# Where the gate's two halves lie in their slot, and the order of the products that read them

## The chip, the cores and the metric

The kernel runs on one core of a Trainium2 chip. Its metric is the device time of one execution in microseconds (us). Before the change three runs took 2553.76, 2554.19 and 2555.51 us; the median is 2554.19 us. The profile shown here is of a separate execution that took 2554.62 us.

## The reference

The program does two things one after the other, in float32. First a spectral layer on x of shape 8 x 3008 x 256: a Fourier transform along the 3008 positions, a complex 256 x 256 mix of the channels with a bias, a soft threshold, and the transform back. Then a feed-forward layer on the 24,064 resulting tokens:

```
h = x @ w_in                      # 256 -> 2048
relu6 = np.clip(h + 3.0, 0.0, 6.0)
g = h * relu6 / 6.0               # the gate
out = g @ w_out                   # 2048 -> 256
```

The change is in the last line of this layer, `g @ w_out`.

## The kernel before, in words

To keep float32 precision on TensorE the kernel splits both factors of most matrix products in two: a high part (the value rounded to the type `float32r`) and a low part (what is left). One product is then three matmuls that add into the same PSUM bank: weights low times data high, weights high times data high, weights high times data low. `product` (L133) writes these three in one of two orders. With `later=True` the matmul on the low part of the data comes last. Without it, it is the second of the three.

The tokens are cut into 47 chunks of T = 512 and the 2048 hidden features into 8 blocks of 256, which gives 376 units (a chunk and a block each). A unit goes through these steps, interleaved with those of its neighbours and with the spectral layer's work for later chunks (lists of slots written before the loop decide what is laid where, and `in_order` and `behind` hold some of it in that order; the rest is ordered by the framework's scheduler):

- the products with `w_in` on 256 columns of tokens (`block`, data in `yb`, weights in `w_in_hi` and `w_in_lo`, results in `pb` and `ps_a`). A Strassen-like scheme turns 8 of them into 7;
- the gate (`gate`, L1077 to L1106): ScalarE computes relu(h + 3) (L1099), VectorE min(.., 6) * h into `r` (L1101), ScalarE rounds `r` to the high part (L1104, two instructions of 512 columns), VectorE subtracts to get the low part (L1105, one instruction of 1024 columns);
- four groups of the products with `w_out` (`down`, L1108): for each of the two halves u of the block and the two halves dh of the 256 outputs one group of three matmuls on 512 columns, with the data in `gs` and the sums in `po`. All 8 blocks of a chunk add into the same two banks.

`gate_parts` (L1077) makes the slot of `gs`: 4T + 64 elements of 4 bytes in each partition, two such slots in turn. In it the high part starts at element 60 (byte 240) and the low part at element 2T + 60 (byte 4336). Both are 112 bytes past a multiple of 128.

In the program as built, the two slots of `gs` and all slots of `yb` start at multiples of 128 bytes; so do the moving operands of the products with `w_in`. The weights `w_in` and `w_out` start 64 bytes past such a multiple, and since a block of 128 weights has 512 bytes, so does each block. For two other groups of three matmuls on 512 columns: `z` (both parts) starts 64 bytes past, with the weights `g64` on a multiple; `xs` (both parts) starts on a multiple, with the weights `f47` 32 and 96 bytes past.

Of the kernel before, what the change touches and what calls it, by code (L numbers as in the profile page):

```python
# [32 lines left out]
T = 512  # L33
# [68 lines left out]
def spectral_ffn(ctx: ExitStack, tc: tile.TileContext, x, w_r, w_i, bias, w_in, w_out, f47, f64, g64, g64u, sgn, out):  # L102
# [11 lines left out]
    def space(shape, dt, name, tag=None):  # L114
        tag = tag or name
        return sb.tile(shape, dt, name=name, tag=tag, bufs=depth.get(tag, 1))
# [16 lines left out]
    def product(ps, terms, start=True, stop=True, more=False, later=False):  # L133

        todo = [p for (ah, al), (bh, bl) in terms for p in (((al, bh), (ah, bh), (ah, bl)) if later else ((al, bh), (ah, bl), (ah, bh)))]
        for n, (a, b) in enumerate(todo):
            nc.tensor.matmul(  # L137
                out=ps,
                lhsT=a,
                rhs=b,  # L140
                start=start and n == 0,
                stop=stop and n == len(todo) - 1,
                skip_group_check=more,
            )
# [590 lines left out]
    def part(pair, sl):  # L735
        return tuple(t[:, sl] for t in pair)
# [339 lines left out]

    def gate_parts(i):  # L1077

        starts = 60, 2 * T + 60
        t = space([P, 4 * T + 64], F32R, "gs")  # L1080
        return [t[:, at : at + 2 * T].rearrange("p (u c) -> p u c", u=2) for at in starts]

    def gate(i):

        h = hs.pop(i)
        if i == len(units) - 1:
            r = space([P, 2, T], F32, "r")
            t = gs[i] = gate_parts(i)
            for u in (1, 0):
                nc.scalar.activation(out=r[:, u], in_=h[:, u], func=AF.Relu, bias=three, scale=1.0)  # L1090
                nc.vector.scalar_tensor_tensor(
                    out=r[:, u], in0=r[:, u], scalar=6.0, in1=h[:, u], op0=ALU.min, op1=ALU.mult
                )
                split(t[0][:, u], t[1][:, u], r[:, u])
            yield
            return
        r = space([P, 2, T], F32, "r")
        for u in range(2):
            nc.scalar.activation(out=r[:, u], in_=h[:, u], func=AF.Relu, bias=three, scale=1.0)  # L1099
        yield  # L1100
        nc.vector.scalar_tensor_tensor(out=r, in0=r, scalar=6.0, in1=h, op0=ALU.min, op1=ALU.mult)  # L1101
        t = gs[i] = gate_parts(i)
        for u in range(2):
            nc.scalar.copy(out=t[0][:, u], in_=r[:, u])  # L1104
        nc.vector.tensor_tensor(out=t[1], in0=r, in1=t[0].bitcast(F32), op=ALU.subtract)  # L1105
        yield  # L1106

    def down(i, u, dh):  # L1108
        c, f = units[i]
        ft = 2 * f + u  # L1110
        ends = i == len(units) - 1
        first, last = f == 0 and u == 0, f == nf - 1 and u == (0 if ends else 1)
        if first:
            pos[dh] = ps_o.tile([P, 512], F32, name=f"po{dh}")
        g = gs[i]
        product(
            pos[dh],
            later=True,
            terms=[(part(wout_s, slice(ft * D + dh * P, ft * D + (dh + 1) * P)), (g[0][:, u], g[1][:, u]))],
            start=first,  # L1120
            stop=last,
        )
        if last:
            ot = space([P, T], F32, "ot")
            if ends and dh:
                for n, at in enumerate((slice(0, H), slice(H, T))):
                    if n:
                        nc.vector.tensor_scalar(
                            out=ot[:, at], in0=pos[dh][:, at], scalar1=1.0 / 6.0, scalar2=None, op0=ALU.mult
                        )  # L1130
                    else:
                        nc.scalar.mul(out=ot[:, at], in_=pos[dh][:, at], mul=1.0 / 6.0)
                    nc.sync.dma_start(
                        out=out[dh * P : (dh + 1) * P, c * T + n * H : c * T + (n + 1) * H], in_=ot[:, at]
                    )
                return
            if dh:
                nc.vector.tensor_scalar(out=ot, in0=pos[dh], scalar1=1.0 / 6.0, scalar2=None, op0=ALU.mult)
            else:
                nc.scalar.mul(out=ot, in_=pos[dh], mul=1.0 / 6.0)  # L1140
            nc.sync.dma_start(out=out[dh * P : (dh + 1) * P, c * T : (c + 1) * T], in_=ot)
# [134 lines left out]
    def group(i, at):  # L1276
        if 0 <= i < n:
            down(i, *order(i)[at])
# [71 lines left out]
```

## Time and profile before

| | |
|---|---|
| median of three runs | 2554.19 us |
| the profiled execution | 2554.62 us |
| its span, first to last instruction | 2552.8 us |
| PE (TensorE matmul) busy | 2532.1 us, 99% |
| DVE (VectorE) busy | 1958.1 us, 77% |
| ACT (ScalarE) busy | 1955.7 us, 77% |
| matmuls on `gs` (L137, into `po`) | 4512, 38% of the chain that ended last |

How to read it: a matmul's record begins when it starts and ends some time after the next one has begun, since matmuls are pipelined. The price of a matmul is therefore the distance from its start to the next start, not the length of its record. In a timeline, rows of the same kind are merged ("x2"), and the starts are given to 0.01 us; over a group of three or six matmuls that is fine enough.

### The profile page before, as it was taken

The numbers are of one execution on the slowest core, as the hardware profiler recorded it, in microseconds if no ns is written. First come the engines' busy times: TensorE is split into PE (matmuls) and PEld (weight loads), VectorE is DVE, ScalarE is ACT, GpSimd is POOL, SyncE is SP. The second block draws the span as 40 slices with busy tenths as digits, with TensorE's granted clock in tenths as the row PEclk, the third lists the DMA queues.
The fourth block names the chain that finished last, engine by engine and source line by source line (L and its number), as shares of the span: only waits on it lengthen the run. The fifth ranks groups of instructions, "written<-read, shape, count | busy, mean of one in ns | idle before, by whom it ended". The sixth has DMA issues, their size and how long they took to land.

```text
span 2552.8 us, 45563 instructions
## 1 busy us (share of the span) xinstructions
PE 2532.1 (99%) x16510; PEld 2260.0 (89%) x16510; DVE 1958.1 (77%) x3176; ACT 1955.7 (77%) x4329; POOL 738.3 (29%) x716
## 2 busy tenths in 40 slices
PE   9999999999999999999999999999999999999999
PEld 6788889899999889988899888998989999998988
DVE  6988877777777877777777777777777877777676
ACT  5777777777777777777777777777777777777877
POOL 2223423343133331433313432134311221121210
PEclk9999999999999999999999999999999999999999
DMA  8534422232122221232212322222311121110000
GB/s 277 174 101 134 132 74 72 82 95 75 56 83 80 89 81 52 81 84 80 82 55 77 92 88 67 65 78 82 91 60 60 56 70 54 37 32 25 20 17 17
DMA packets 147321, 199.75 MB, mean 78 GB/s; under 512 B 16319, under 2 KB 102039, under 8 KB 147095
## 3 DMA queue, kind: packets, MB, share of 16 engines
q1 hardware_dynamic: 147095, 196.83, 25.5%
q8 instruction: 130, 2.13, 0.3%
q14 instruction: 96, 0.79, 0.1%
HBM read 99.77 MB, written 74.97 MB: 68 GB/s over the span
## 4 chain that ended last, share of the span: by engine, by line
PE 89%; DVE 4%; ACT 3%; issue 2%; DMA 1%; POOL 0%; SPq 0%; DVEq 0%; ACTq 0%; POOLq 0%
PE po L137 38%; PE ps_a L137 24%; PE pb L137 19%; PE ps_a L871 3%; PE ps_a L757 2%; PE ps_a L472 1%; DVE gs L1105 1%; ACT gs L1104 1%; DVE r L1101 1%; DVE h L1014 1%; ACT r L1099 1%; DMA xin<-in_x 1%; PE ps_a L507 0%; PE pb L438 0%; DVE tc L796 0%
## 5 line engine op out<-in xcount | busy, mean ns | idle before, releaser
L137 PE MATMUL po<-gs,w_out_hi 128*128 128x512 f32 x3008 | 948.1, 395 | 1.1 <-DVE gs L1105 1.0
L1099 ACT ACTIVATE r<-h,three 128x512 f32<-128x512 f32 x750 | 541.7, 726 | 147.5 <-DVE h L1014 132.4
L1101 DVE SCALAR_TENSOR_TENSOR r<-r,h 128x1024 f32<-128x1024 f32 x375 | 491.0, 1309 | 212.6 <-ACT r L1099 211.7
L137 PEld LDWEIGHTS po<-gs,w_out_hi 128*128 128x128 f32 x3008 | 564.8, 188 | 89.4 <-DVE gs L1105 5.4
L137 PE MATMUL po<-gs,w_out_lo 128*128 128x512 f32 x1504 | 613.6, 408 | 0.5 <-ACT ot L1140 0.2
L1105 DVE TENSOR_TENSOR gs<-r,gs 128x1024 fp32r<-128x1024 f32 x375 | 478.9, 1277 | 161.6 <-ACT gs L1104 161.1
L1104 ACT CAST gs<-r 128x512 fp32r<-128x512 f32 x750 | 430.7, 622 | 185.3 <-DVE r L1101 180.1
L137 PE MATMUL pb<-yb,w_in_hi 128*128 128x256 f32 x3004 | 555.2, 278 | 0.0
L137 PEld LDWEIGHTS pb<-yb,w_in_hi 128*128 128x128 f32 x3004 | 455.9, 188 | 32.9
L131 POOL TENSOR_TENSOR yb<-T,yb 128x256 fp32r<-128x256 f32 x184 | 195.9, 1067 | 835.4 <-ACT yb L130 835.2
L137 PE MATMUL ps_a<-yb,w_in_hi 128*128 128x256 f32 x2252 | 426.1, 278 | 0.0
L137 PE MATMUL pb<-yb,w_in_lo 128*128 128x256 f32 x1502 | 419.7, 280 | 3.4 <-ACT u L1011 1.8
L1014 DVE TENSOR_TENSOR h<-ps_a,u 128x256 f32<-128x256 f32 x752 | 313.7, 417 | 112.3 <-PE ps_a L137 109.8
L137 PEld LDWEIGHTS ps_a<-yb,w_in_hi 128*128 128x128 f32 x2252 | 342.3, 188 | 15.8 <-DVE yb L131 0.2
L1011 ACT COPY u<-pb 128x256 f32<-128x256 f32 x752 | 279.7, 373 | 91.2 <-PE pb L137 89.4
L137 PE MATMUL ps_a<-yb,w_in_lo 128*128 128x256 f32 x1126 | 315.4, 280 | 5.1 <-DVE h L1014 4.9
L137 PEld LDWEIGHTS pb<-yb,w_in_lo 128*128 128x128 f32 x1502 | 282.4, 188 | 41.6 <-ACT u L1011 3.7
L137 PEld LDWEIGHTS po<-gs,w_out_lo 128*128 128x128 f32 x1504 | 283.7, 189 | 20.8 <-issue 2.3
L137 PEld LDWEIGHTS ps_a<-yb,w_in_lo 128*128 128x128 f32 x1126 | 211.7, 188 | 30.2 <-DVE h L1014 13.3
L1011 ACT COPY p<-pb 128x256 f32<-128x256 f32 x376 | 138.7, 369 | 30.9 <-PE pb L137 28.9
L1014 DVE TENSOR_TENSOR h<-ps_a,p 128x256 f32<-128x256 f32 x376 | 156.3, 416 | 2.1 <-ACT p L1011 1.4
L131 POOL TENSOR_TENSOR xs<-xin,xs 120x512 fp32r<-120x512 f32 (+1 forms) x42 | 55.9, 1331 | 305.0 <-ACT xs L130 305.0
(189 smaller groups left out, 3446.0 us busy)
## 6 DMA issues: line engine op xcount, KB each, us to landing
xin<-in_x SPq DMA_DIRECT2D x48, 512.0 KB, 3.7
bt<-scr SPq DMA_DIRECT2D x96, 256.0 KB, 3.1
scr<-pt SPq DMA_DIRECT2D x96, 256.0 KB, 2.0
out<-ot SPq DMA_DIRECT2D x93, 256.0 KB, 2.0
scr<-a SPq DMA_DIRECT2D x96, 240.0 KB, 2.5
qt<-scr SPq DMA_DIRECT2D x96, 240.0 KB, 3.5
zt<-tc SPq DMA_DIRECT2D x336, 64.0 KB, 2.0
f<-in_f SPq DMA_DIRECT2D x96, 128.0 KB, 2.9
```

The lines of the kernel that those rows point to most:

```text
L131: (on or nc.vector).tensor_tensor(out=lo, in0=src, in1=hi.bitcast(F32), op=ALU.subtract)
L137: nc.tensor.matmul(out=ps, lhsT=a, rhs=b, start=start and n == 0, stop=stop and n == len(todo) - 1, skip_group_check=more,)
L472: nc.tensor.matmul(out=to, lhsT=x[:, xh, dh, which], rhs=w_s[w][wh][:, dh * D : (dh + 1) * D], start=False, stop=n == 2 and (which, dh) == ...
L757: nc.tensor.matmul(out=psv[:, dh, :, u, :], lhsT=data[:, u, dh * P : (dh + 1) * P], rhs=f[:, u, :], start=True, stop=True,)
L871: nc.tensor.matmul(out=ps[:, cs * w + g * rows : cs * w + (g + 1) * rows], lhsT=qt[:rows, cs, g, dh * P : (dh + 1) * P], rhs=f47_s[2][:row ...
L1011: nc.scalar.copy(out=t, in_=ps)
L1014: nc.vector.tensor_tensor(out=hs[i][:, u, half * H : (half + 1) * H], in0=ps, in1=keep.pop((i, n)), op=ALU.add)
L1099: nc.scalar.activation(out=r[:, u], in_=h[:, u], func=AF.Relu, bias=three, scale=1.0)
L1101: nc.vector.scalar_tensor_tensor(out=r, in0=r, scalar=6.0, in1=h, op0=ALU.min, op1=ALU.mult)
L1104: nc.scalar.copy(out=t[0][:, u], in_=r[:, u])
L1105: nc.vector.tensor_tensor(out=t[1], in0=r, in1=t[0].bitcast(F32), op=ALU.subtract)
```

## The change

The high part now starts at element 2T + 64 (byte 4352, a multiple of 128) and the low part at element 16 (byte 64). The call in `down` no longer asks for `later=True`, so the matmul on the low part is the second of the three.

```diff
     def gate_parts(i):
 
-        starts = 60, 2 * T + 60
+        starts = 2 * T + 64, 16
         t = space([P, 4 * T + 64], F32R, "gs")
         return [t[:, at : at + 2 * T].rearrange("p (u c) -> p u c", u=2) for at in starts]
 
@@ in down(i, u, dh)
         product(
             pos[dh],
-            later=True,
             terms=[(part(wout_s, slice(ft * D + dh * P, ft * D + (dh + 1) * P)), (g[0][:, u], g[1][:, u]))],
             start=first,
             stop=last,
```

The orders of the three matmuls of a group, weights first:

```
before: low x high, high x high, high x low
after:  low x high, high x low,  high x high
```

The program's list of instructions names both parts `gs`, so most groups read alike before and after ("w_out_hi x2"). What does show is where the scheduler puts other matmuls between those of a group, at the start, near the end and at a few places between. On TensorE at the first groups of the program (`po_1359` and `po_1385` are the banks of the two output halves of the first chunk):

```order
 L137 MATMUL po_1359<-gs,w_out_lo 128x512
-L137 MATMUL po_1359<-gs,w_out_hi 128x512
+L137 MATMUL po_1385<-gs,w_out_lo 128x512
 L137 MATMUL ps_a<-yb,w_in_lo 128x256
 L137 MATMUL ps_a<-yb,w_in_hi 128x256 x2
@@ -244,6 +244,5 @@
 L137 MATMUL pb<-yb,w_in_hi 128x256 x2
 L137 MATMUL ps_a<-yb,w_in_hi 128x256
-L137 MATMUL po_1359<-gs,w_out_hi 128x512
-L137 MATMUL po_1385<-gs,w_out_lo 128x512
+L137 MATMUL po_1359<-gs,w_out_hi 128x512 x2
 L137 MATMUL po_1385<-gs,w_out_hi 128x512 x2
```

Before, a group's first two matmuls stood ahead of the products on `yb`, and its last, on the low part, behind them; now only the first stands ahead, joined by the first of the next group. On TensorE at the last chunk (`po_30486` and `po_30508` are its two banks):

```order
 L137 MATMUL po_30486<-gs,w_out_lo 128x512
-L137 MATMUL po_30486<-gs,w_out_hi 128x512
 L137 MATMUL po_30508<-gs,w_out_lo 128x512
-L137 MATMUL po_30508<-gs,w_out_hi 128x512
-L137 MATMUL po_30486<-gs,w_out_hi 128x512
-L137 MATMUL po_30508<-gs,w_out_hi 128x512
+L137 MATMUL po_30486<-gs,w_out_hi 128x512 x2
+L137 MATMUL po_30508<-gs,w_out_hi 128x512 x2
 L137 MATMUL po_30486<-gs,w_out_lo 128x512
 L137 MATMUL po_30486<-gs,w_out_hi 128x512 x2
```

Here four matmuls could run on the weights low part and the data's high part before the data's low part was needed; now two can.

## Rows read from the trace of the kernel before

**Rows 1.** The page: busy time of each engine, its share of the span, instructions.

```profile
PE 2532.1 (99%) x16510; PEld 2260.0 (89%) x16510; DVE 1958.1 (77%) x3176; ACT 1955.7 (77%) x4329; POOL 738.3 (29%) x716
```

**Rows 2.** Cores: span and mean granted TensorE clock.

```profile
core 0: 2552.8 us, clock 1.000
```

**Rows 3.** The page: the chain that ended last, share of the span by line.

```profile
PE po L137 38%; PE ps_a L137 24%; PE pb L137 19%; PE ps_a L871 3%; PE ps_a L757 2%; PE ps_a L472 1%; DVE gs L1105 1%; ACT gs L1104 1%; DVE r L1101 1%; DVE h L1014 1%; ACT r L1099 1%; DMA xin<-in_x 1%; PE ps_a L507 0%; PE pb L438 0%; DVE tc L796 0%
```

**Rows 4.** Groups by line: xcount, busy us, mean ns, then idle before them.

```profile
L137 PE MATMUL po<-gs,w_out_hi 128*128 128x512 f32 x3008 | 948.1, 395 | 1.1 <-DVE gs L1105 1.0
L137 PE MATMUL po<-gs,w_out_lo 128*128 128x512 f32 x1504 | 613.6, 408 | 0.5 <-ACT ot L1140 0.2 <-ACT gs L1104 0.2
L137 PE MATMUL pb<-yb,w_in_hi 128*128 128x256 f32 x3004 | 555.2, 278 | 0.0
L137 PE MATMUL ps_a<-yb,w_in_hi 128*128 128x256 f32 x2252 | 426.1, 278 | 0.0
L137 PE MATMUL pb<-yb,w_in_lo 128*128 128x256 f32 x1502 | 419.7, 280 | 3.4 <-ACT u L1011 1.8 <-ACT p L1011 1.4
L137 PE MATMUL ps_a<-yb,w_in_lo 128*128 128x256 f32 x1126 | 315.4, 280 | 5.1 <-DVE h L1014 4.9
```

**Rows 5.** Tile yb: duration ns min/median/max, first and last start.

```profile
L137 PE MATMUL pb<-yb,w_in_hi x3004: 276/276/290, 105.3 to 2542.3; 128*128 128x256 f32 x188
```

**Rows 6.** Timeline of PE, a fast stretch: start us, length us, instruction.

```profile
1607.04 0.28 PE L137 MATMUL pb<-yb,w_in_lo 128*128 128x256 f32 x1
...
1607.72 0.40 PE L137 MATMUL po<-gs,w_out_lo 128*128 128x512 f32 x1
1607.95 0.63 PE L137 MATMUL po<-gs,w_out_hi 128*128 128x512 f32 x2
1608.42 0.28 PE L137 MATMUL ps_a<-yb,w_in_lo 128*128 128x256 f32 x1
```

**Rows 7.** Timeline of PE, a group on z and what follows.

```profile
1602.41 0.28 PE L137 MATMUL ps_a<-yb,w_in_lo 128*128 128x256 f32 x1
...
1602.75 0.39 PE L137 MATMUL ps_a<-z,g_lo 128*128 128x512 f32 x1
...
1603.44 0.39 PE L137 MATMUL po<-gs,w_out_lo 128*128 128x512 f32 x1
...
1604.14 0.28 PE L137 MATMUL pb<-yb,w_in_lo 128*128 128x256 f32 x1
...
1605.20 0.39 PE L137 MATMUL po<-gs,w_out_lo 128*128 128x512 f32 x1
```

**Rows 8.** Timeline of PE, a group on gs in a slow stretch.

```profile
1621.13 0.39 PE L137 MATMUL po<-gs,w_out_lo 128*128 128x512 f32 x1
...
1621.82 0.28 PE L137 MATMUL ps_a<-yb,w_in_lo 128*128 128x256 f32 x1
```

**Rows 9.** Timeline of PE, a group on xs.

```profile
1515.25 0.40 PE L137 MATMUL ps_a<-xs,f_lo 120*120 120x512 f32 x1
...
1515.95 0.39 PE L137 MATMUL po<-gs,w_out_lo 128*128 128x512 f32 x1
```

**Rows 10.** Line L1105, the low part: who waited for it (us, times).

```profile
  PEld po L137: 5.4, 14
  PE po L137: 1.0, 3
```

**Rows 11.** Tiles gs and z: VectorE's subtraction of 512 columns, ns min/median/max.

```profile
L131 DVE TENSOR_TENSOR gs<-r,gs x2: 684/688/693, 2546.1 to 2546.9; 128x512 fp32r<-128x512 f32 x2
L131 DVE TENSOR_TENSOR z<-zt,z x84: 676/692/1822, 197.9 to 2209.6; 128x512 fp32r<-128x512 f32 x84
```

**Rows 12.** Timeline of PE and PEld near the end, the last wait for a low part.

```profile
2543.49 0.40 PE L137 MATMUL po<-gs,w_out_lo 128*128 128x512 f32 x1
...
2543.96 0.39 PE L137 MATMUL po<-gs,w_out_lo 128*128 128x512 f32 x1
...
2544.46 0.30 PEld L137 LDWEIGHTS po<-gs,w_out_hi 128*128 128x128 f32 x2 [0.31 <-DVE gs L1105]
```

## The prediction, made before the changed kernel ran

> **What bounds the kernel now.** I read the busy line first: TensorE is busy for 2532.1 of 2552.8 us, VectorE and ScalarE for 77% each [rows 1]. The granted clock is 1.000, so all of it runs at the upper of the clock's two levels, 2.4 GHz [rows 2]. Next the chain that ended last: its largest share, 38%, are the products into `po`, the ones that the change touches, and 43% more are those on 256 columns into `ps_a` and `pb` [rows 3]. In the groups by line the reader is to see how little these matmuls wait: 1.6 us before all 4512 products on `gs` [rows 4]. So the time is set by the distance from one matmul's start to the next, and a change can act in two ways only: through that distance or through a new wait.
>
> The third view, the timeline, gives the distance. There are two kinds of stretch. In a fast one, two groups of three on `yb` take 1607.72 − 1607.04 = 0.68 us, that is 113.3 ns a matmul of 256 columns, and the group on `gs` behind them takes 1608.42 − 1607.72 = 0.70 us [rows 6]. In a slow one, nine matmuls on `yb` take 1605.20 − 1604.14 = 1.06 us, 117.8 ns each [rows 7], and a group on `gs` takes 0.69 us [rows 8]. Nothing waits in either; the pace itself differs, by 4.5 ns on 256 columns. How much of the kernel is fast follows from the records: the shortest and the median record on `yb` are both 276 ns [rows 5] and the mean is 278 [rows 4]. If a slow matmul's record is 4.5 ns longer, 2 / 4.5 = 44% are slow and 56% fast.
>
> **The change part by part.** *Nothing is added.* As many matmuls, weight loads, casts and subtractions are issued, with the same shapes, and no DMA moves.
>
> *The new places, seen from TensorE.* In a fast stretch a group on `gs` has 2 x 768 columns, and two groups on `yb` with as many columns take 0.68 us, not 0.70 [rows 6]. What differs is where the moving data start: `yb` on a multiple of 128 bytes, `gs` 112 past, with the weights 64 past for both. After the change the high part lies as `yb` does. I take it that a group then keeps `yb`'s pace: 0.02 us less for each of 1504 groups in the fast 56%, 1504 x 0.56 x 0.02 = 16.8 us. For slow stretches I take no gain: `yb`'s slow pace would make 6 x 117.8 = 0.707 us of a group that now takes 0.69. The low part lies as neither does. The nearest row is `z`, whose two parts start 64 past, though with weights on a multiple: 1603.44 − 1602.75 = 0.69 us [rows 7]. The bounds of this term are therefore a loss of 1504 x 0.56 x 0.007 = 6 us (a group at the slow pace of 0.707) and a gain of 1504 x 0.02 = 30 us (all groups at 0.68, slow ones included).
>
> *The pace behind a group.* Whether a stretch is fast or slow seems to depend on what ran before it. Ahead of the group on `z` three matmuls on `yb` took 0.34 us, behind it and one group on `gs` nine took 1.06 [rows 7]; behind groups on `gs` alone the fast pace stays [rows 6]. I take the split of 56 to 44 as unchanged. The bounds: all 7884 matmuls on `yb` [rows 4] slow, 7884 x 0.56 x 4.5 ns = 19.9 us more, or all fast, 7884 x 0.44 x 4.5 ns = 15.6 us less.
>
> [...]
>
> *The places, seen from the writers.* ScalarE and VectorE write the parts at the new starts. VectorE's subtraction of 512 columns takes 688 ns into `gs`, 112 past, and 692 into `z`, 64 past [rows 11]: no price. Were there one of 4 ns in each 512 columns, it would lie beside TensorE's work, for both engines are idle 23% of the time.
>
> *The order.* The subtraction's result is now needed by the second matmul of a group, not the third. TensorE has waited for it 3 times in all and its weight loads 14 times [rows 10], at the start and the end. The framework's scheduler has moved other matmuls into most of these gaps, as the rows of the order show; where it has none, one product of 0.235 us stands behind the wait that stood ahead. On the last chunk two do: before the wait of 0.31 us there were four products, 0.235 us apart (0.47 us for two, 2543.49 to 2543.96) [rows 12], and now there are two, so 0.47 us more. Queued behind are all later matmuls of the chunk. Bounds: 0 and 17 x 0.235 = 4.0 us; I take 1.0, the end and two more.
>
> The sum, against the profiled execution: 2554.62 − 16.8 + 1.0 = 2538.8 us. It took 0.43 us more than the median of the runs shown, so **2538 us** on their scale, 0.6% less.
>
> **The rivals.**
>
> *A. Forecast and larger gain.* The same mechanism, from 2538 down to where slow stretches vanish too: 2554.2 − 30 − 15.6 + 1 = 2510 us. For it: the only moving operand that keeps 113.3 ns for long is one on a multiple of 128 with weights 64 past, and two of the three matmuls now have that. Against it: the low part between them does not.
>
> *B. The place is not what sets the pace.* A group on `xs` starts on a multiple of 128 and takes 1515.95 − 1515.25 = 0.70 us [rows 9], one on `z` 0.69: none is at 0.68. Then only the order is left: 2554.2 + 1.0 = 2555 us, and with small gains 2552. Against it: their weights lie at other places (32, 96 and 0), so the pair is not the same. The Trainium skill (SBUF — State Buffer, "Specifications") has a rule that speaks for this rival: lines of SBUF have 16 bytes, and a price is paid for crossing to a new one. All four starts, 240, 4336, 4352 and 64, are multiples of 16, so by it the time would stay at 2554 us. Against the page stands that `yb` and `gs`, both on multiples of 16, keep a different pace per column.
>
> *C. The low part turns fast stretches slow.* This is the one on the other side. The change of place between neighbours, on a multiple, 64 past, on a multiple, does what the group on `z` does: it takes 0.69 us and leaves a slow stretch behind. Then the fast 56% lose the pace: + 19.9 us on `yb`, − 1504 x 0.56 x 0.01 = − 8.4 us on `gs`, + 1.0 for the order, 2554.2 + 12.5 = 2567 us. It decides as soon as more than 8.4 / 19.9 = 42% of the fast stretches are lost, if groups go to 0.69. For it: rows 7, where the one operand 64 past is followed by the slow pace. Against it: there the weights too lie elsewhere, and the last matmul before `yb` is now one on the high part.
>
> **How the numbers follow.** A has 52%: the forecast 2538 with a range of its own from 2515 to 2549, the larger gain below that. B has 16%. C has 32%, from 2558 to 2575. The range that should hold 8 of 10 reaches from the middle of the larger gain to past C's price: 2514 to 2572 us. A difference under 0.2% (5 us) can't be told from none. Faster by more than that: A without its weakest results and a little of B, 0.52. Within: most of B and the edges of A and C, 0.15. Slower: C, 0.33.
>
> **What would show it.** Right: in the timeline after, a group on `gs` between two on `yb` takes 0.68 us and the matmuls on `yb` keep 0.34 us a group of three; the mean record of the products on `gs` falls by some 4 ns (16.8 us / 4512) while that on `yb` stays at 278. Rival A's lower end: the mean on `yb` falls to 276. B: groups still take 0.70. C: the mean on `yb` rises towards 281, and 117.8 ns appears behind every group. The order is wrong in size if TensorE's waits for L1105 add up to more than 5 us. The forecast fails if the pace of a matmul doesn't depend on where its data start, or if the low part's place undoes what the high part's gives.

## The result, and the profile after

The changed kernel takes 2567.99 us (median of four runs, 2565.64 to 2569.19) against 2554.55 us for the kernel before beside it. The ratio is 1.0053, with a 95% interval of 1.0041 to 1.0065: 0.5% slower. The forecast was 2538 us, faster. The time lies within the range on record, and 1 us from what rival C gave, 2567 us.

The first rows to compare are those that bound the kernel, the clock and TensorE's busy time (cores, and the page's line of busy times, of the changed kernel; before: [rows 1, 2]):

```profile
core 0: 2567.4 us, clock 1.000
PE 2546.3 (99%) x16510; PEld 2282.0 (89%) x16510; DVE 1960.2 (76%) x3176; ACT 1958.6 (76%) x4329; POOL 731.9 (29%) x716
```

The clock is the same and TensorE is again busy for 99%. The span grew by 2567.4 − 2552.8 = 14.6 us, TensorE's busy time by 14.2: the time is in the matmuls themselves, not in waits. Which ones, the groups by line say (changed kernel; columns as in [rows 4]):

```profile
L137 PE MATMUL po<-gs,w_out_hi 128*128 128x512 f32 x3008 | 939.2, 394 | 1.5 <-DVE gs L1105 1.3
L137 PE MATMUL po<-gs,w_out_lo 128*128 128x512 f32 x1504 | 612.3, 408 | 0.2 <-ACT ot L1139 0.2
L137 PE MATMUL pb<-yb,w_in_hi 128*128 128x256 f32 x3004 | 562.4, 280 | 0.0
L137 PE MATMUL ps_a<-yb,w_in_hi 128*128 128x256 f32 x2252 | 431.5, 280 | 0.1
```

Against [rows 4] the products on `gs`, which the change touches, became a little shorter (395 to 394 ns with `w_out_hi`), and those on `yb`, which it does not touch, longer by 2 ns. The tile's own view shows why (tile `yb`, changed kernel; columns as in [rows 5]):

```profile
L137 PE MATMUL pb<-yb,w_in_hi x3004: 275/281/290, 104.9 to 2556.4; 128*128 128x256 f32 x188
```

The shortest record still is 275 ns, but the median has gone from 276 [rows 5] to 281. Where most matmuls on `yb` were fast, most are now slow. From the starts of all matmuls in both traces: 4688 of 7896 on `yb` had at most 115 ns to the next start before, 1219 of 7896 have now. Summed over all starts, the matmuls on `yb` take 16.1 us more, the other products on 256 columns (`X`) 3.5 us more, and those on `gs` 4.7 us less. Together that is 14.9 us, against 14.6 us in the span.

The timeline shows the place where it happens (TensorE, changed kernel: a fast stretch, a group on `gs`, what follows):

```profile
807.27 0.28 PE L137 MATMUL ps_a<-yb,w_in_lo 128*128 128x256 f32 x1
...
807.62 0.28 PE L137 MATMUL ps_a<-yb,w_in_lo 128*128 128x256 f32 x1
...
807.96 0.39 PE L137 MATMUL po<-gs,w_out_lo 128*128 128x512 f32 x1
...
808.64 0.28 PE L137 MATMUL pb<-yb,w_in_lo 128*128 128x256 f32 x1
...
809.70 0.40 PE L137 MATMUL ps_a<-z,g_lo 128*128 128x512 f32 x1
```

Ahead of the group, three matmuls on `yb` take 807.96 − 807.62 = 0.34 us, the fast pace. The group takes 808.64 − 807.96 = 0.68 us: the saving of 0.02 us that the forecast counted on is there. Behind it nine matmuls on `yb` take 809.70 − 808.64 = 1.06 us, the slow pace of [rows 7]. Nothing waits. The pace was lost across the group. The engines that write `gs` at the new places are not what slows it down. Of the matmuls on `yb` that began while ScalarE or VectorE wrote `gs`, 577 of 2525 had the fast pace in the changed kernel, of the others 642 of 5371.

The order's part shows in the waits (line L1105 of the changed kernel, who waited for it, us and times; and PEld near the end, as in [rows 12]):

```profile
  PEld po L137: 4.4, 11
  PE po L137: 1.3, 4
2558.54 0.53 PEld L137 LDWEIGHTS po<-gs,w_out_hi 128*128 128x128 f32 x3 [0.73 <-DVE gs L1105]
```

The last wait grew from 0.31 to 0.73 us, by 0.42 where the forecast had 0.47; over the whole program such waits did not grow (4.4 + 1.3 = 5.7 us against 6.4 [rows 10]).

### The profile page after: what moved, and what is told of

Same layout as the page of the kernel before. It is cut to its first block, busy times and chain, and to the rows that moved or that the text cites. A ratio compares the mean times of both kernels' runs of the same rounds, so it can differ in the third digit from the quotient of the medians.

```text
span 2567.4 us, 45563 instructions
## 1 busy us (share of the span) xinstructions
PE 2546.3 (99%) x16510; PEld 2282.0 (89%) x16510; DVE 1960.2 (76%) x3176; ACT 1958.6 (76%) x4329; POOL 731.9 (29%) x716
## 4 chain that ended last, share of the span: by engine, by line
PE 88%; DVE 4%; ACT 3%; DMA 2%; issue 2%; POOL 0%; SPq 0%; DVEq 0%; ACTq 0%; POOLq 0%
PE po L137 37%; PE ps_a L137 24%; PE pb L137 19%; PE ps_a L871 3%; PE ps_a L757 2%; PE ps_a L472 1%; DVE gs L1105 1%; ACT gs L1104 1%; DVE r L1101 1%; ACT r L1099 1%; DVE h L1014 1%; DMA xin<-in_x 1%; DMA qt<-scr 0%; PE ps_a L507 0%; DVE tc L796 0%
## 5 line engine op out<-in xcount | busy, mean ns | idle before, releaser
L1105 DVE TENSOR_TENSOR gs<-r,gs 128x1024 fp32r<-128x1024 f32 x375 | 481.1, 1283 | 161.4 <-ACT gs L1104 161.1
L137 PE MATMUL pb<-yb,w_in_hi 128*128 128x256 f32 x3004 | 562.4, 280 | 0.0
L137 PE MATMUL ps_a<-yb,w_in_hi 128*128 128x256 f32 x2252 | 431.5, 280 | 0.1
L131 POOL TENSOR_TENSOR yb<-raw,yb 128x256 fp32r<-128x256 f32 x138 | 131.2, 960 | 46.9 <-ACT yb L130 46.9
```

Of the source, the lines that this page charges most:

```text
L131: (on or nc.vector).tensor_tensor(out=lo, in0=src, in1=hi.bitcast(F32), op=ALU.subtract)
L137: nc.tensor.matmul(out=ps, lhsT=a, rhs=b, start=start and n == 0, stop=stop and n == len(todo) - 1, skip_group_check=more,)
```

## The experiments

All times are medians. Ratios are against the kernel before, run beside each. "Low in the middle" is the new order, without `later=True`. The edits are in `gate_parts` where nothing else is said; a place is given as bytes past a multiple of 128.

### Places or order

New places, old order:

```diff
-        starts = 60, 2 * T + 60
+        starts = 2 * T + 64, 16
```

> The new places with the old order (low part last). PLACE theory (the low part at 64 past, beside a high part on a multiple, makes a group that leaves the fast pace): most of the loss is here already, 2562 to 2570 us, the mean record on yb at 280 to 281 ns, a group behind fast yb about 0.68 us. ORDER theory (it is the low part in the middle that breaks the pace): the fast pace stays, 2535 to 2555 us, mean record on yb 278 or below.

Measured: 2567.56 us, ratio 1.0051 (1.0039 to 1.0064). The tile `yb` of this run:

```profile
L137 PE MATMUL pb<-yb,w_in_hi x3004: 276/281/287, 104.5 to 2555.0; 128*128 128x256 f32 x188
```

Old places, new order:

```diff
-            later=True,
```

> The old places (112 past) with the new order. PLACE theory: 2554 to 2557 us, groups behind fast yb still 0.70 us, mean record on yb 278 ns; the order costs only its waits, about 1 us. ORDER theory: the loss is here, 2562 to 2570 us, mean record on yb 280 to 281 ns.

Measured: 2556.79 us, 1.0009 (1.0000 to 1.0018), and on `yb`:

```profile
L137 PE MATMUL pb<-yb,w_in_hi x3004: 276/276/287, 104.2 to 2543.7; 128*128 128x256 f32 x188
```

The median record is 281 with the new places alone and 276 with the new order alone. The places carry the loss. The order costs about 2 us, with an interval that reaches down to nothing. ORDER has fallen. One expectation of mine was off: a group behind fast `yb` takes 0.70 us in the first run, not 0.68; the shorter group needs the new order as well.

### Both parts at one place

```diff
+        starts = 0, 2 * T
```

> New order, both parts on a multiple of 128 (bytes 0 and 4096), as yb lies. PLACE theory in its strict form (all three moving operands at yb's place keep yb's pace): groups of 0.68 us and the fast pace stays behind them, 2520 to 2540 us, mean record on yb 276 to 278. Rival LENGTH (the fast pace stays only behind a group of 0.70 us and is lost behind any shorter one, whatever its places): groups of 0.68 us, but yb slow, 2562 to 2570 us, mean record on yb 280 to 281.

Measured: 2559.28 us, 1.0017 (1.0008 to 1.0026). The strict form of PLACE has fallen: the three matmuls lie as `yb` does and still do not keep its pace. A group behind fast `yb` takes 692 ns, not 680, so LENGTH, which expected 0.68, did not hold in its form either. This bears on the forecast too: data at `yb`'s place did not give a group `yb`'s pace.

```diff
+        starts = 16, 2 * T + 16
```

> New order, both parts 64 past a multiple of 128 (bytes 64 and 4160), as z lies. PLACE theory: 64 past is the harmful place, so the fast pace is lost, 2560 to 2572 us, mean record on yb 280 to 281. Rival CHANGE (it is the change of place from one matmul to the next within the group that breaks the pace, not a place): the pace stays, 2535 to 2557 us, mean record on yb 278 or below.

Measured: 2559.13 us, 1.0018 (1.0009 to 1.0026), between the two ranges. The pace on `yb` is lost as PLACE had it, with no change of place inside a group, so CHANGE has fallen; but the groups gain. TensorE's timeline in this run, a slow stretch, a group, a slow stretch:

```profile
185.21 0.28 PE L137 MATMUL ps_a<-yb,w_in_lo 128*128 128x256 f32 x1
...
185.57 0.39 PE L137 MATMUL po<-gs,w_out_lo 128*128 128x512 f32 x1
...
186.25 0.28 PE L137 MATMUL pb<-yb,w_in_lo 128*128 128x256 f32 x1
...
187.31 0.28 PE L137 MATMUL ps_a<-w_r_hi,X 128*128 128x256 f32 x1
```

The group takes 186.25 − 185.57 = 0.68 us in the middle of a slow stretch (1.06 us for nine on `yb` behind it). Summed over all starts, `gs` is 15.8 us cheaper than before and `yb` 18.0 us dearer. So 0.68 us a group is to be had, and a gain on `gs` can be paid back on `yb`.

### Data against weights

`yb` moved 64 bytes, other tiles left at their places modulo 128, with the parts 64 past, then with the old places and the new order:

```diff
+    pads = {'yb': 16, 'r': 16}
...
+        if tag in pads:
+            sb.tile([P, pads.pop(tag)], F32, name='pad' + tag, tag='pad' + tag, bufs=1)
...
+        starts = 16, 2 * T + 16    # the second kernel: 60, 2 * T + 60
```

> Both parts of the gate 64 past, and all of yb 64 past too (it lay on multiples; nothing else changes its place modulo 128). GRID theory: matmuls keep the short pace on a grid of 6.67 ns, each place of the data has its own phase on it, and where neighbours lie at the same place the pace passes from one to the other. Then both kinds keep it: groups of 0.68 us and yb at 113.3 ns nearly throughout, 2554 - 30 - 16 = about 2510 us (2505 to 2535), mean record on yb 276 to 277. Rival PAIR (yb keeps its pace only because it lies 64 bytes from its weights' place): yb at 64 with weights at 64 loses it, 2555 to 2575 us, mean record on yb 281.

> The gate's parts at the old places (112 past), new order, yb 64 past. GRID theory: yb keeps 113.3 ns by itself, but its phase is another, so a group of 0.70 us need not end on it: between 2545 and 2572 us. Rival PAIR: yb is slow throughout, 2565 to 2580 us, mean record on yb 281, no stretch at 113.3 ns.

Measured: 2579.38 us, 1.0102 (1.0088 to 1.0115), and 2580.28 us, 1.0104 (1.0090 to 1.0117). My GRID theory expected 2510 of the first and was 70 us off; it also had 2572 as the most for the second. PAIR forecast the slow pace in both, with its upper ends 4 and 0.3 us too low. With `yb` and `w_in` both 64 past, only 439 and 155 of the 7896 matmuls on `yb` are fast. The place of `yb` sets its pace. Whether its distance from the weights' place is the reason, as PAIR had it, these two runs do not show, since `w_in` stayed where it was.

`w_out` moved 64 bytes to a multiple, with two tiles of 16 elements around it, and both parts on a multiple:

```diff
+    const.tile([P, 16], F32, name='pad1')
     wout_s = [const.tile([P, NFT * D], F32R, name="w_out_" + t) for t in ("hi", "lo")]
+    const.tile([P, 16], F32, name='pad2')
...
+        starts = 0, 2 * T
```

> Both parts of the gate on a multiple of 128, and w_out moved by 64 bytes to a multiple too, so that data and weights of the groups lie at one place, as in the run with both parts 64 past. Rival PAIR (the difference between the places of data and weights sets the pace): groups at 0.68 us, mean record of the products on gs with w_out_hi at 389 to 391, as in that run. Against it, PLACE alone (the weights do not matter): as with both parts on a multiple and the old weights, mean record 394, 2557 to 2561 us.

Measured: 2561.39 us, 1.0031 (1.0019 to 1.0042), mean record 393 with `w_out_hi`, between the two expectations. PAIR does not hold in this form: data and weights lie at one place, and a group behind fast `yb` takes 700 ns, not 680. PLACE alone does not hold either. With the weights at their old place and the same data the group took 692 ns, and 46% of the matmuls on `yb` were fast against 24% here. So the weights' place counts. The run is also the exception in the table below.

### Other places for both parts

```diff
+        starts = 16, 2 * T + 64    # high 64 past, low on a multiple
```

> The change with the two places exchanged: high part 64 past, low part on a multiple of 128, new order. If it is the mixture of two places within a group that breaks the pace: as the change, 2562 to 2572 us, mean record on yb 280 to 281. If the place of the last matmul alone decides: as with both parts 64 past, about 2559 us, with groups near 0.68 us.

Measured: 2565.51 us, 1.0051 (1.0037 to 1.0065), in the range given for a mixture. The time alone does not make the mixture the cause: both parts at one place lost the pace as well (the runs before), and some mixtures further on keep it.

```diff
+        starts = 16, 2 * T + 60    # high 64 past, low 112 past; later=True kept
```

> High part 64 past, low part 112 past (the old place), old order (low part last). From the pitches of the earlier runs, a group behind fast yb should take 278 + 279 + 275 cycles of 1.2 GHz = 693 ns, which is 104 steps of 6.67 ns. GRID-END theory (the fast pace survives a group that ends on a whole step, as the old one of 700 ns does): the fast share stays, about 2554 - 836 x 0.007 = 2548 us (2543 to 2557), mean record on yb 278. Rival (the last matmul of a group must come at the phase and behind the pitch that it has with both parts 112 past): fast share lost, 2560 to 2570 us, mean record on yb 280 to 281.

Measured: 2575.26 us, 1.0087 (1.0073 to 1.0100). I had put the group at 693 ns by adding pitches from other runs; it takes 701.6. The pitches do not add up that way, and so the run says little about GRID-END by its own condition: 701.6 ns is not a whole number of steps.

```diff
+        starts = 8, 2 * T + 8      # 32 past; 24: 96 past; 12: 48 past
```

> Both parts 32 past, new order. If only multiples of 64 behave specially: as with 112 past, 2554 to 2558 us. If each place has its own pitches, and the end of the group against the 6.67 ns grid decides: anywhere from 2530 to 2570 us, with the time following the mean record on yb (each ns of it about 7.9 us) and the length of a group (each 0.01 us about 15 us if all change).

> Both parts 96 past, new order. The same two expectations as for 32 past; 32 and 96 differ by 64, as 0 and 64 do, so if the place counts modulo 64 alone the two agree within 3 us; if modulo 128, they may differ by 5 us or more.

> Both parts 48 past, new order; 48 and 112 differ by 64. If the place counts modulo 64 alone: 2555 to 2558 us, as with both parts 112 past and the new order, mean record on yb 278. If it counts modulo 128: another split, 2560 us or more.

Measured: 32 past 2574.27 us, 1.0079 (1.0065 to 1.0093); 96 past 2563.28 us, 1.0035 (1.0023 to 1.0048); 48 past 2566.34 us, 1.0046 (1.0034 to 1.0059). The first is 4 us above the wider of its two ranges. 32 and 96 differ by 11 us, and 48 and 112 (2556.79) by 10: places 64 bytes apart are not alike. Whether places 128 bytes apart are alike, no run tested.

### The two moves of the change apart

```diff
+        starts = 2 * T + 64, 60    # high part moved, low part left
```

> New order, the high part moved to byte 4352 (a multiple of 128), the low part left 112 past (byte 240). LOW theory (the low part at 64 past ends the fast pace, as the prediction's third rival had it): most of the fast pace is kept, mean record on yb 278, 2535 to 2558 us. Rival ANY (every place but 112 past for all three data operands ends the fast pace): fast pace kept behind fewer than half of the groups, mean record on yb 280 or more, 2560 to 2572 us.

Measured: 2544.36 us, 0.9961 (0.9949 to 0.9974): **faster than before**. LOW was right here and ANY wrong.

```diff
+        starts = 2 * T + 60, 16    # low part moved, high part left
```

> New order, the low part moved to byte 64, the high part left 112 past (byte 4336). LOW theory: 2562 to 2572 us, mean record on yb 280 to 281. Rival HIGH (the high part on a multiple does it): 2553 to 2558 us, mean record on yb 278. Rival ANY: 2560 to 2572 us, as in the run before.

Measured: 2575.32 us, 1.0080 (1.0066 to 1.0094). The time is slow as LOW said, 3 us above its range, yet not for its reason: the mean record on `yb` stays at 278. HIGH has fallen. TensorE's timeline of this run:

```profile
193.43 0.28 PE L137 MATMUL ps_a<-yb,w_in_lo 128*128 128x256 f32 x1
...
193.77 0.40 PE L137 MATMUL po<-gs,w_out_lo 128*128 128x512 f32 x1
...
194.50 0.28 PE L137 MATMUL pb<-yb,w_in_lo 128*128 128x256 f32 x1
...
194.85 0.28 PE L137 MATMUL pb<-yb,w_in_lo 128*128 128x256 f32 x1
...
195.53 0.40 PE L137 MATMUL po<-gs,w_out_lo 128*128 128x512 f32 x1
```

Here the group itself is long, 194.50 − 193.77 = 0.73 us, and after three matmuls on `yb` (0.35 us) the fast pace is back: 195.53 − 194.85 = 0.68 us for six. The low part at 64 past is dear beside a high part 112 past, and ends the pace beside a high part on a multiple. Against the old places with the new order the two moves alone make −12.4 and +18.5 us, together 6.1, but the change made 2568 − 2556.8 = 11.2: they do not add.

Every second unit at the new places:

```diff
+        starts = (2 * T + 64, 16) if i % 2 else (60, 2 * T + 60)
```

> New order; every second unit (and so one of the two slots of gs) has the new places, the others the old ones. GROUP theory (each group passes the pace on or ends it, and it can return only behind a group at the old places): behind groups at the old places the fast pace stays and returns as in the kernel before, behind groups at the new ones it ends; the time is about midway between the old places with the new order and the change, (2556.8 + 2568) / 2 = 2562 us (2558 to 2565), mean record on yb 279 to 280. Rival WHOLE (the pace is set by something common to the whole program, its placement of all data): near one end, 2553 to 2557 or 2566 to 2570 us.

Measured: 2560.91 us, 1.0024 (1.0014 to 1.0033), inside what GROUP expected. Counted as in the table below, groups at the old places passed the fast pace on 103 of 106 times and brought it back 61 of 157 times; groups at the new places passed it on 10 of 123 times and brought it back 3 of 128 times. The loss is made group by group, where the new places are.

### Whether the end of a group decides

```diff
+        starts = 2 * T + 64, 20    # high on a multiple, low 80 past; 24: 96 past; 12: 48 past
```

> New order, high part on a multiple of 128, low part 80 past. GRID-END theory: if a group behind fast yb lasts a whole number of 6.67 ns steps (680.0 or 686.7 ns) the fast pace is kept behind 9 of 10 groups, mean record on yb 278 or less, 2535 to 2550 us; if not, it is lost, 280 to 281, 2560 to 2572 us. Rival ONLY-64 (64 past is the harm): kept whatever the length of the group, 2535 to 2555 us.

> The same with the low part 96 past: GRID-END, kept if the group lasts a whole number of steps (2535 to 2550 us) and lost if not (2560 to 2572 us); ONLY-64, kept whatever its length.

> The same with the low part 48 past, 64 before the place that keeps the pace: GRID-END, kept if the group lasts a whole number of steps (2535 to 2550 us) and lost if not (2560 to 2572 us); ONLY-64, kept whatever its length.

Measured: low 80 past **2535.87 us, 0.9929 (0.9917 to 0.9942)**; 96 past 2554.55 us, 1.0005 (0.9996 to 1.0013); 48 past 2573.12 us, 1.0075 (1.0061 to 1.0089). The first is the fastest kernel of this study, 0.7% under the kernel before. The second is below the 2560 us that GRID-END had for a lost pace: the pace is lost behind nearly every group there, but comes back behind the next one. The groups by line and the timeline of the first, to be held against those of the changed kernel above:

```profile
L137 PE MATMUL po<-gs,w_out_hi 128*128 128x512 f32 x3008 | 933.6, 392 | 2.8 <-DVE gs L1105 2.7
L137 PE MATMUL pb<-yb,w_in_hi 128*128 128x256 f32 x3004 | 552.0, 277 | 0.0
```

```profile
347.02 0.28 PE L137 MATMUL ps_a<-yb,w_in_lo 128*128 128x256 f32 x1
...
347.36 0.39 PE L137 MATMUL po<-gs,w_out_lo 128*128 128x512 f32 x1
...
348.04 0.28 PE L137 MATMUL pb<-yb,w_in_lo 128*128 128x256 f32 x1
...
349.06 0.39 PE L137 MATMUL po<-gs,w_out_lo 128*128 128x512 f32 x1
```

The group takes 0.68 us here too, but the nine matmuls behind it take 349.06 − 348.04 = 1.02 us, not 1.06. The two kernels differ by 16 bytes in the place of the low part.

In the timeline both groups read 0.68 us. The starts of all records tell them apart. The table counts, in each trace, the groups on `gs` that stand alone, with at least two matmuls on `yb` ahead and six behind. The pace is fast where the pitch is at most 115 ns (one pitch ahead; the mean of the third to fifth behind). The length is the mean over groups behind fast `yb` within 4 ns of their median, and a step is 6.667 ns, the longest that goes a whole number of times into both the fast pitch and the group of the kernel before: 113.33 ns are 17 steps, 700.0 ns are 105. "Kept": fast ahead and fast behind, of those fast ahead. "Back": slow ahead and fast behind, of those slow ahead.

```
high/low, order      length ns   steps   kept      back      fast on yb   us
112/112 last (before)   700.0   105.00   279/291    97/225      59%     2554
112/112 middle          700.0   105.00   272/285    95/229      59%     2557
  0/80  middle          680.0   102.00   451/467    29/47       81%     2536
  0/112 middle          686.7   103.00   323/341   125/173      70%     2544
 32/32  middle          693.3   104.00    82/90     51/424      25%     2574
112/64  middle          728.3   109.25   421/437    58/77       61%     2575
  0/64  middle (change) 679.1   101.87     7/119     7/395      15%     2568
  0/96  middle          679.2   101.89     9/244   255/270      41%     2555
  0/0   middle          692.5   103.87    14/276   207/238      46%     2559
 64/64  middle          695.0   104.25     2/72     18/442      12%     2559
  0/48  middle          695.1   104.27    10/143     9/371      17%     2573
 48/48, 96/96 middle    697.5   104.63    21/570   302/458    40, 50%   2566, 2563
  0/64  last            698.5   104.77     0/24      9/492      22%     2568
 64/112 last            701.6   105.24     1/143    87/373      23%     2575
 64/0   middle          705.0   105.74     6/161   175/353      24%     2566
  0/0   middle, w_out 0 699.9   104.98     0/97      4/417      24%     2561
```

Of the fifteen rows with the weights in their old place, the five whose groups last a whole number of steps keep the fast pace behind nine groups of ten or more. Nine of the other ten lose it nearly always; one, 112/64, keeps it through a detour: its group and the three matmuls behind it take 194.85 − 193.77 = 1.08 us together, which is 162 steps again (1080.0 ns in the mean over such groups). ONLY-64 has fallen, since 96 and 48 past lose the pace too. The last row is a real exception: with `w_out` moved, groups of 105 steps lose it. So with the weights where they are, keeping the pace went with a whole step, and that is not a rule for all weights. Keeping it is not enough for a fast kernel: 32/32 keeps it 82 of 90 times, but brings it back only 51 of 424 times and takes 2574 us.

That the step is the cause is not shown. No run set a group's length without moving its data or its weights or changing its order, and two counts speak against it as the whole cause. In the trace of 0/80, 28 groups behind fast `yb` miss a whole step by more than 1 ns, most of them by a pause inside, and 21 of these keep the pace. In the changed kernel, 954 of 957 starts inside fast stretches fall in the same seven tenths of a step, counted from the first instruction; 107 of the 119 groups behind fast `yb` end in these tenths too, and 5 of the 107 keep the pace.

## Why the prediction was wrong

**The bound** was right: the time is the distance between starts, and 14.2 of the 14.6 us came through it, as TensorE's busy time.

**The new places, a group's own length** (−16.8 us): the length came out and the reason did not. Groups behind fast `yb` went from 700 to 679 ns, as forecast. But the forecast took this from the high part lying as `yb` does, and with both parts there a group took 692 ns, with the same places as the change in the old order 698.5: that 679 matched was in part luck. And only 130 of 674 groups or rows of groups still began in a fast stretch, where before it were 410 of 679, so that `gs` gained 4.7 us in all. So few fast stretches follow from the next step.

**The pace behind a group** is the step that failed: "I take the split of 56 to 44 as unchanged." The fast share of `yb` went from 59% to 15%, and the matmuls on `yb` took 16.1 us more, against my bound of 19.9 for all of them slow; 3.5 us more on `X`, which the sum did not have, make it 19.6. I had the term at nothing because the fast pace stays behind groups on `gs` [rows 6], but that row shows it for the old places alone, the ones that the change took away. I had split the change into a saving inside the group and a split of paces outside, as if the second did not depend on the first. The runs show that it does: behind groups at the old places the fast pace stayed 279 of 291 times, behind groups at the new ones 7 of 119 times, and with the two kinds in one program the loss was made at the new places. What goes with it is the length, 105.00 steps before and 101.87 after. [rows 6] held half of this: 113.3 ns a matmul and 0.70 us a group are 17 and 105 steps of 6.667 ns. They would not have settled it, since the forecast 0.68 us is 102 steps, a whole number, and the group came out 0.9 ns shorter. It came out at 102 steps with the low part 16 bytes further on. That kernel's 2535.87 us are near the forecast's 2538, but not by its terms: against the trace before, `gs` takes 11.9 us less, not 16.8, and `yb` 5.1 us less, not the same.

**The low part.** I had bounded it by `z` and took it that the group keeps `yb`'s pace by its high part. Moving the high part alone gave 2544 us, the low part alone 2575. With the high part on a multiple the low part's place alone made anything from 2535.87 us (80 past) to 2573.12 (48 past); but 64 past ends the pace there and keeps it beside a high part 112 past, so it is the two places together that count.

**Rival C** named the result (2567 us) and the loss of the fast pace, with + 19.9 on `yb` (measured 16.1, and 3.5 on `X`, which it did not count) and − 8.4 on `gs` (measured − 4.7). That the total came within 1 us is in part luck: its groups were to take 0.69 us and took 0.68 behind fast `yb`. Its cause, a change of place between neighbours, does not hold in general: the two fastest kernels, 0/80 and 0/112, change the place twice in each group.

**Rival B** is out: with the order kept, the places alone made 13 us. One of its counter-arguments was weaker than it read: in the program as built, half of the groups on `xs` have their weights on a multiple (low part) and 64 past (high part), not 32 and 96. The Trainium skill (SBUF — State Buffer, "Specifications") tells of lines of 16 bytes. All places tried are multiples of 16, and the times run from 2535.87 to 2580.28 us, so here more than that line counts.

**The order** (+1.0 us): by itself 2.3 us (0 to 4.6 by its interval), which holds the forecast, with the last wait 0.42 us longer. That waits are its price is not shown, for with the new order alone those on L1105 add up to 6.2 us. My sign for a wrong size, waits on L1105 of more than 5 us, was a poor one, for with the weight loads they were 6.4 us before.

**Not settled:** why a group lasts a whole step at some pairs of places and not at others, whether that length is what keeps the pace, and what in the weights' place undoes it. The runs show it as a table of lengths, not as a mechanism.

## What to carry to other kernels

Where TensorE never waits, compare the starts of matmuls, not their records, and look at the instructions behind those that were changed: a group that is 3% shorter can leave its neighbours 4% slower. Before a place in memory is moved, scan a few places beside it (16 bytes made 32 us here) and move one operand at a time. And a term that "stays as it is" needs a row that shows it for the changed kernel's conditions, not for those of before: here it stood in the sum as nothing, and it was the whole answer.

## What the runs showed of the hardware that was not expected

- With the clock at 1.000 throughout, matmuls of 256 columns run at 113.3 or about 117.8 ns with no wait between them, and which of the two holds is mostly passed on: in the kernel before, across 279 of 291 groups behind a fast stretch, while 128 of 225 behind a slow one stayed slow.
- The place of the data matters to 16 bytes (2567.99 us with the low part 64 past, 2535.87 with it 80 past), and so does that of the weights (with both parts on a multiple, groups of 692 ns with weights 64 past and 700 on a multiple). `yb` on a multiple with weights 64 past is fast in 59% of its matmuls in the kernel before, 64 past with the same weights in 2 to 6%.
- The same group of three matmuls on 512 columns took from 679 to 728 ns behind fast `yb`, by the place of its data and the order of its matmuls.
